# Channel mix after pooled attention: transposing the probabilities of tiles 6 to 35 as 32 by 32 blocks on VectorE, with on-chip transfers, instead of on TensorE

## The chip, the core and the metric

The kernel runs on one core of one Trainium2 chip. The metric is device time in microseconds (us). TensorE (PE in the profile, PEld for its weight loads) multiplies matrices, VectorE (DVE), ScalarE (ACT) and GpSimd (POOL) work on elements, and SyncE (SP) issues transfers. Each engine takes its own instructions strictly in order; an instruction that has to wait holds up all that stand behind it on its engine.

## The reference: what is computed

Eight batches of 576 tokens, 8 heads of width 64. Keys and values are averaged over groups of 8, so each head has 72 keys. Then attention, and a channel mix over the 512 attended features of each token and of the token before it:

```python
k_p = k.reshape(B, H, Sp, pool, D).mean(axis=3)
v_p = v.reshape(B, H, Sp, pool, D).mean(axis=3)
scores = scale * np.matmul(q, k_p.transpose(0, 1, 3, 2))
attn = softmax(scores)
x = np.matmul(attn, v_p)             # heads side by side: 8 x 576 x 512
xk = mu_k * x + (1.0 - mu_k) * x_prev
xr = mu_r * x + (1.0 - mu_r) * x_prev
k = np.maximum(xk @ w_k, 0.0)
v = k * k @ w_v
r = 1.0 / (1.0 + np.exp(-(xr @ w_r)))
out = r * v
```

## The kernel before

The 4608 tokens are cut into 12 chunks of 384 tokens, each of 3 tiles of 128 tokens: 36 tiles, numbered from 0. Line numbers here are those of the profile of the kernel before.

**Per tile.** `softmax` makes scores on TensorE (L592) into the one `sc` bank of PSUM, takes the maximum, subtracts, exponentiates on ScalarE (L628), sums and inverts on VectorE (L605 to L636), and multiplies by the inverse on GpSimd. It makes two tiles of this: `px` (L642), the last 8 keys of each head, and `pm` (L648), the first 64. The attention product needs the keys on the partitions. `transposed` does that for `pm` with four 128 by 128 TensorE transposes into a PSUM bank (L667), from which ScalarE copies a rounded high part `pth` (L678) and VectorE makes the low part `ptl` by subtraction (L680). `transposed_rest` spreads `px` on VectorE into three parts (L698, L700), transposes them with two TensorE instructions (L706), and ScalarE copies the result to `ptr` (L713).

**Per chunk.** `attended` (L749) multiplies values with `pth`, `ptl` and `ptr` into PSUM; `shifted` and `x_parts` make the mixed inputs `xkh`, `xkl`, `xrh`, `xrl` (L762 to L799). `hidden` (L825) multiplies with `w_k` in 8 groups, each into one of three `mm` banks that ScalarE (`rk`, `sh`) and VectorE (`rk`, `sl`) empty; `gate` (L874) multiplies with `w_r`, `mixed` (L906) with `w_v`, and each tile of outputs goes to memory from SyncE (L922). Except in chunk 0 each product is made of three matmuls, high with high, low with high, high with low. `pth`, `ptl` and `ptr` have one buffer each: a tile of chunk c may be written there only once chunk c-1 has been attended.

**What sets the order.** All steps are generators. `Order.run` plays them against a rough model of engine times and buffer slots, and records the instructions in the order in which this planner starts them; a step may begin when what it `need`s is `made` and the slot that it `take`s is free, and among the ready steps of an engine the one with the earliest due time wins. Attention steps on TensorE are held back by a `spare` of 3.0 us from chunk 2 on. `EARLIER` shifts single due times. The chip follows that order, whatever the times turn out to be. SyncE's one list holds all loads of queries, keys and values and the output stores.

Of the kernel before, what the change touches and what calls it, by code (L numbers as in the profile page):

```python
# [191 lines left out]
def attention_then_channel_mix(  # L192
# [60 lines left out]
    slots("xm", 3, [P, CH])  # L253
    slots("rk", 2, [P, CH])
    slots("e", 2, [P, 2, 4, KEYS])
    slots("pm", 2, [P, 2, 4, KM])
    slots("px", 2, [P, 2, 4, KR])
    slots("pr", 2, [P, 2, 3, 4, KR], F32R)
    slots("mx", 2, [P, 2, 4, 1])
    slots("sm", 2, [P, 2, 4, 1])  # L260
    slots("vq", 1, [REM, 2, D], F32R)
    slots("tmp", 2, [P, WP])
    slots("qs", 3, [P, NPAIR, P])
    slots("stage", 3, [P, 2 * POOL * KEYS])

# [63 lines left out]

    def warm():  # L330

        zeros = yield take("tmp")
        yield "dve", 0.5, False
        nc.vector.memset(zeros, 0.0)
        bank = yield take("bank")
        for _ in range(WARMING):
            yield "pe", 0.86, False
            nc.tensor.matmul(out=bank[:, :256], lhsT=zeros[:, :P], rhs=zeros[:, :256], start=True, stop=True)
        order.give("bank", bank)
        order.give("tmp", zeros)  # L340
# [74 lines left out]
    def convert(kind, i):  # L415

        yield need(("w" + kind, i))  # L420
        got = held.pop(("got", kind, i))
        w = got.rearrange("p (n two) -> p n two", two=2)
        low_word, top = w[:, :, 0], w[:, :, 1]
        ff = yield take("tmp")
        t = ff.bitcast(I32)
        yield act(WP)
        nc.scalar.activation(out=ff, in_=top.bitcast(F32), func=AF.Abs)
        yield "dve", 0.335, True
        nc.vector.tensor_scalar(out=ff, in0=ff, scalar1=TINY, scalar2=None, op0=ALU.max)  # L429
# [6 lines left out]
        nc.vector.scalar_tensor_tensor(  # L436
            out=t, in0=top, scalar=-0x40000000, in1=t, op0=ALU.bitwise_and, op1=ALU.bitwise_or
        )
        yield dve(WP)
        full[kind, i] = got[:, :WP].bitcast(F32)  # L440
        nc.vector.scalar_tensor_tensor(
            out=got[:, :WP], in0=low_word, scalar=29, in1=t,
            op0=ALU.logical_shift_right, op1=ALU.bitwise_or,
        )
        order.give("tmp", ff)
        order.make(("full", kind, i))

    order_of = [w[1:] for w in LOADS.split() if w[0] == "w"]
# [123 lines left out]
    def softmax(i):  # L572
# [61 lines left out]
            out=sm, in0=sm, scalar1=1e-9, scalar2=float(POOL), op0=ALU.add, op1=ALU.mult  # L634
        )
        nc.vector.reciprocal(out=sm, in_=sm)  # L636
# [5 lines left out]
        eng.tensor_tensor(  # L642
            out=px, in0=e[:, :, :, KM:], in1=sm.broadcast_to([P, 2, 4, KR]), op=ALU.mult
# [6 lines left out]
        )  # L650
        order.give("e", e)
        order.give("sm", sm)
        held["pm", i] = pm
        order.make(("pm", i))

    def transposed(i):
        c, off, _ = tiles[i]
        o = slice(off, off + P)
        yield need(("pm", i), *([("attended", c - 1)] if c else []))
        if c == 1:  # L660
            yield need(("early", "ptl", 0))
        pm = held.pop(("pm", i))
        bank = yield take("bank")
        tp = bank.rearrange("p (a b) -> p a b", b=P)
        yield "pe", 0.44, False
        for g in range(NPAIR):
            nc.tensor.transpose(  # L667
                out=tp[:, g, :],
                in_=pm[:, g // 2, (g % 2) * 2:(g % 2) * 2 + 2, :].rearrange("p h k -> p (h k)"),
                identity=ident,  # L670
            )
        order.give("pm", pm)
        yield act(NPAIR * P)
        if c in WHOLE:
            nc.scalar.copy(out=operand("pth", c)[:, :, o], in_=tp)
        else:
            pt_h, pt_l = operand("pth", c), operand("ptl", c)
            nc.scalar.copy(out=pt_h[:, :, o], in_=tp)  # L678
            yield dve(NPAIR * P, False)
            nc.vector.tensor_tensor(  # L680
                out=pt_l[:, :, o], in0=tp, in1=pt_h[:, :, o], op=ALU.subtract
            )
# [327 lines left out]
```

## Time and profile before

| | us |
|---|---|
| median of 3 runs (lowest, highest) | 635.99 (635.57, 636.23) |
| the profiled execution | 637.05 |
| its span, first to last instruction | 635.3 |
| TensorE busy | 621.9 |
| VectorE busy | 413.9 |
| ScalarE busy | 334.4 |
| GpSimd busy | 215.8 |

The 1.75 us between the span and the profiled execution lie around the program. Matmuls are pipelined, so the profile's time of one (277 ns for a transpose) is longer than what it adds to TensorE; what it adds is read from the starts of the instructions around it. "PE L667 x4" in a timeline is four instructions in a row of one line.

### The profile page before, as it was taken

The numbers are of one execution on the slowest core, as the hardware profiler recorded it, in microseconds if no ns is written. First come the engines' busy times: TensorE is split into PE (matmuls) and PEld (weight loads), VectorE is DVE, ScalarE is ACT, GpSimd is POOL, SyncE is SP. The second block draws the span as 40 slices with busy tenths as digits, with TensorE's granted clock in tenths as the row PEclk, the third lists the DMA queues.
The fourth block names the chain that finished last, engine by engine and source line by source line (L and its number), as shares of the span: only waits on it lengthen the run. The fifth ranks groups of instructions, "written<-read, shape, count | busy, mean of one in ns | idle before, by whom it ended". The sixth has DMA issues, their size and how long they took to land.

```text
span 635.3 us, 9068 instructions
## 1 busy us (share of the span) xinstructions
PE 621.9 (98%) x3256; PEld 538.6 (85%) x3256; DVE 413.9 (65%) x830; ACT 334.4 (53%) x688; POOL 215.8 (34%) x331
## 2 busy tenths in 40 slices
PE   7899999999999999999999999999999999999997
PEld 6754468889989989989988988988988988988986
DVE  5999998856979537647845665855854654653421
ACT  4667656855665644645454555546555455444420
POOL 1240348464435128028115018316405105203100
PEclk9999999999999999999999999999999999999999
DMA  9991130043314111033011061033110100000001
GB/s 293 364 390 62 33 125 35 15 126 142 91 51 172 61 35 51 0 142 108 17 35 51 0 202 49 16 109 125 33 34 34 35 17 34 18 0 35 18 0 50
DMA packets 35132, 50.91 MB, mean 80 GB/s; under 512 B 6544, under 2 KB 23184, under 8 KB 35088
## 3 DMA queue, kind: packets, MB, share of 16 engines
q1 hardware_dynamic: 34944, 50.22, 23.5%
q8 instruction: 25, 0.41, 0.3%
q14 instruction: 19, 0.16, 0.1%
q10 hardware_dynamic: 144, 0.13, 0.1%
HBM read 40.90 MB, written 9.44 MB: 79 GB/s over the span
## 4 chain that ended last, share of the span: by engine, by line
PE 84%; DMA 6%; DVE 5%; POOL 2%; SPq 1%; issue 1%; ACT 0%; DVEq 0%; POOLq 0%; ACTq 0%
PE mm L906 28%; PE mm L825 28%; PE mm L874 15%; PE bank L749 5%; PE sc L592 4%; DMA qs<-in_qT 4%; PE bank L667 2%; DMA got_wv<-in_w_v 1%; DMA got_wr<-in_w_r 1%; PE bank L706 1%; DVE tmp L436 1%; SPq L397 1%; POOL xkl L799 0%; DVE tmp L429 0%; POOL w_r L466 0%
## 5 line engine op out<-in xcount | busy, mean ns | idle before, releaser
L825 PE MATMUL mm<-xkh,w_k 128*128 128x384 f32 x704 | 182.2, 339 | 0.3 <-ACT xkh L797 0.3
L906 PE MATMUL mm<-w_v,sh 128*128 128x512 f32 x528 | 170.8, 392 | 0.0
L825 PEld LDWEIGHTS mm<-xkh,w_k 128*128 128x128 f32 x704 | 125.6, 188 | 1.5 <-issue 0.6
L825 PE MATMUL mm<-xkl,w_k 128*128 128x384 f32 x352 | 118.1, 336 | 0.7 <-POOL xkl L799 0.7
L906 PEld LDWEIGHTS mm<-w_v,sh 128*128 128x128 f32 x528 | 99.2, 188 | 19.8 <-issue 0.2
L906 PE MATMUL mm<-w_v,sl 128*128 128x512 f32 x264 | 103.0, 390 | 0.0
L642 POOL TENSOR_TENSOR px<-e,sm 128x64 f32<-128x64 f32 x32 | 11.4, 356 | 225.3 <-DVE sm L636 225.2
L874 PE MATMUL mm<-w_r,xrh 128*128 128x512 f32 x264 | 84.9, 394 | 0.0
L762 ACT ACTIVATE t<-bank,om_sb 128x384 f32<-128x384 f32 x96 | 48.8, 582 | 56.2 <-PE bank L749 56.1
L848 ACT CAST sh<-rk 128x384 fp32r<-128x384 f32 x88 | 45.2, 514 | 58.2 <-DVE rk L842 58.1
L781 DVE SCALAR_TENSOR_TENSOR xm<-bank,mu_sb,t 128x384 f32<-128x384 f32 x88 | 51.4, 612 | 35.2 <-POOL t L774 18.3
L850 DVE TENSOR_TENSOR sl<-rk,sh 128x384 fp32r<-128x384 f32 x88 | 53.5, 611 | 25.6 <-ACT sh L848 25.6
L825 PEld LDWEIGHTS mm<-xkl,w_k 128*128 128x128 f32 x352 | 66.1, 188 | 1.3 <-POOL xkl L799 1.3
L920 DVE TENSOR_TENSOR rs<-mm,rs 128x512 f32<-128x512 f32 (+1 forms) x37 | 24.8, 673 | 61.4 <-PE mm L906 61.4
L842 DVE SCALAR_TENSOR_TENSOR rk<-mm,rk 128x384 f32<-128x384 f32 x88 | 48.5, 553 | 16.4 <-ACT rk L835 15.8
L874 PEld LDWEIGHTS mm<-w_r,xrh 128*128 128x128 f32 x264 | 49.6, 188 | 10.0
L799 POOL TENSOR_TENSOR xkl<-xm,xkh 128x384 fp32r<-128x384 f32 x44 | 44.8, 1021 | 37.0 <-ACT xkh L797 36.6
L906 PEld LDWEIGHTS mm<-w_v,sl 128*128 128x128 f32 x264 | 49.7, 188 | 9.0
L473 POOL TENSOR_TENSOR stage<-stage 128x512 f32<-128x512 f32 (+5 forms) x60 | 51.0, 857 | 14.1 <-DMA stage<-in_vm 6.6
L835 ACT ACTIVATE rk<-mm 128x384 f32<-128x384 f32 x88 | 42.9, 488 | 23.3 <-PE mm L825 22.7
L874 PE MATMUL mm<-w_r,xrl 128*128 128x512 f32 x132 | 51.4, 389 | 0.0
L605 DVE TENSOR_REDUCE mx<-sc 128x8 f32<-128x576 f32 x35 | 26.3, 752 | 31.4 <-PE sc L592 31.4
(117 smaller groups left out, 979.2 us busy)
## 6 DMA issues: line engine op xcount, KB each, us to landing
out<-rs SPq DMA_DIRECT2D x35, 256.0 KB, 2.0
stage<-in_kT SPq DMA_DIRECT2D x15, 576.0 KB, 5.0
qs<-in_qT SPq DMA_DIRECT2D x32, 256.0 KB, 3.2
stage<-in_vm SPq DMA_DIRECT2D x14, 512.0 KB, 6.5
got_wk<-in_w_k SPq DMA_DIRECT2D x8, 512.0 KB, 9.2
got_wv<-in_w_v SPq DMA_DIRECT2D x8, 512.0 KB, 10.0
stage<-in_vr SPq DMA_DIRECT2D x7, 384.0 KB, 4.1
got_wr<-in_w_r SPq DMA_DIRECT2D x4, 512.0 KB, 8.3
```

The lines of the kernel that those rows point to most:

```text
L473: nc_eng.tensor_tensor(out=st[:, :, :w], in0=st[:, :, :w], in1=st[:, :, w:2 * w], op=ALU.add)
L749: nc.tensor.matmul(out=xp[:, o], lhsT=v, rhs=p, start=(q == 0), stop=(q == len(terms) - 1))
L762: nc.scalar.activation(out=t[:, m, 1:n + 1], in_=xp, func=AF.Copy, scale=om_sb[:, m, g:g + 1])
L781: nc.vector.scalar_tensor_tensor(out=xm[:, :n], in0=xp, scalar=mu_sb[:, m, g:g + 1], in1=t[:, m, :n], op0=ALU.mult, op1=ALU.add,)
L799: nc.gpsimd.tensor_tensor(out=lo, in0=xm[:, :n], in1=hi, op=ALU.subtract)
L825: nc.tensor.matmul(out=hp, lhsT=w[:, o], rhs=x[:, ct, :n], start=(ct == 0 and k == 0), stop=(ct == NCT - 1 and k == len(terms) - 1),)
L835: nc.scalar.activation(out=rk[:, :n], in_=hp, func=AF.Relu)
L842: nc.vector.scalar_tensor_tensor(out=rk[:, :n], in0=hp, scalar=0.0, in1=rk[:, :n], op0=ALU.max, op1=ALU.mult)
L848: nc.scalar.copy(out=sh[:, :n], in_=rk[:, :n])
L850: nc.vector.tensor_tensor(out=operand("sl", c)[:, jt, :n], in0=rk[:, :n], in1=sh[:, :n], op=ALU.subtract)
L874: nc.tensor.matmul(out=bank, lhsT=x[:, ct, o], rhs=w, start=(ct == 0 and k == 0), stop=(ct == NCT - 1 and k == len(terms) - 1),)
L906: nc.tensor.matmul(out=bank, lhsT=s[:, o], rhs=w, start=(jt == 0 and k == 0), stop=(jt == NJT - 1 and k == len(terms) - 1),)
```

## The change

For tiles 6 to 35, from the first tile of chunk 2 on, `transposed` and `transposed_rest` are not run. GpSimd multiplies all 72 keys of `e` in place in one instruction. A new step, `turned`, lets VectorE transpose 32 by 32 blocks in three instructions into `u` (in a slot of kind `pm`), and SyncE then issues 16 transfers from SBUF to SBUF, 4 for each quarter of the partitions, which put the blocks where a whole transpose would have put them, in `d` (a slot of kind `tmp`, of which there are two). Twelve of the transfers hold 32 rows of 512 bytes, four hold 32 rows of 768 bytes. A new step, `split_turned`, waits for the transfers and for chunk c-1 to be attended; ScalarE copies `pth` and twice a part of `ptr` out of `d`, VectorE subtracts for `ptl` and for the third part of `ptr`. Then `d` is free again. Only `warm` and `convert` are edited otherwise, for the new shape of `tmp`. The `EARLIER` entries for `transposed_rest 6` and `transposed_rest 8` have no step left to shift.

The core of the diff (renamings for the larger `pm` and `tmp` slots left out):

```diff
+TURNED = 6
+BLOCK = 32
...
-    slots("pm", 2, [P, 2, 4, KM])
+    slots("pm", 2, [P, 2 * 4 * KEYS])
...
-    slots("tmp", 2, [P, WP])
+    slots("tmp", 2, [P, P // BLOCK, 6 * BLOCK])
...
         eng = nc.vector if v else nc.gpsimd
+        if i >= TURNED:
+            yield dve(8 * KEYS) if v else pool(8 * KEYS)
+            eng.tensor_tensor(out=e, in0=e, in1=sm.broadcast_to([P, 2, 4, KEYS]), op=ALU.mult)
+            order.give("sm", sm)
+            yield from turned(i, e)
+            return
...
+    at_of = [0, 6 * BLOCK, 10 * BLOCK, 14 * BLOCK, 18 * BLOCK]
+
+    def turned(i, e):
+        u = yield take("pm")
+        yield "dve", 0.8, False
+        pairs = e.rearrange("p a (h two) k -> p (a h) two k", two=2)
+        for h2 in range(2):
+            lo, hi = at_of[2 * h2], at_of[2 * h2 + 2]
+            if h2 == 0:
+                hi = 2 * at_of[1]
+            nc.vector.transpose(
+                out=u[:, lo:hi].rearrange("p (f n) -> p f n", f=2)[:, :, :4 * BLOCK].rearrange(
+                    "p f (g j) -> p f g j", j=BLOCK
+                ),
+                in_=pairs[:, :, h2, :KM].rearrange("p g (f j) -> p f g j", j=BLOCK),
+            )
+        nc.vector.transpose(
+            out=u[:, 4 * BLOCK:6 * BLOCK].rearrange("p (r h k) -> p r h k", r=2, k=KR), in_=e[:, :, :, KM:]
+        )
+        order.give("e", e)
+        d = yield take("tmp")
+        for a in range(P // BLOCK):
+            yield "sp", 1.6, False
+            for c in range(4):
+                nc.sync.dma_start(
+                    out=d[c * BLOCK:(c + 1) * BLOCK, a, :at_of[c + 1] - at_of[c]],
+                    in_=u[a * BLOCK:(a + 1) * BLOCK, at_of[c]:at_of[c + 1]],
+                )
+        held["turned", i] = d
+        order.fetched(("turned", i), 400)
+        order.now += 3.0
+        order.give("pm", u)
...
+    def split_turned(i):
+        c, off, _ = tiles[i]
+        yield need(("turned", i), ("attended", c - 1))
+        d = held.pop(("turned", i))
...
+        yield act(NPAIR * P)
+        nc.scalar.copy(out=pt_h, in_=main)
+        yield act(2 * P)
+        nc.scalar.copy(out=ptr[:rows], in_=rest)
+        yield dve(NPAIR * P)
+        nc.vector.tensor_tensor(out=pt_l, in0=main, in1=pt_h, op=ALU.subtract)
+        order.make(("main", i))
+        yield dve(2 * P)
+        nc.vector.tensor_tensor(out=ptr[rows:2 * rows], in0=rest, in1=ptr[:rows], op=ALU.subtract)
+        yield act(2 * P)
+        nc.scalar.copy(out=ptr[2 * rows:], in_=rest)
+        order.give("tmp", d)
+        order.make(("side", i))
...
+        if i >= TURNED:
+            order.add(tile_due[i] + 0.1, split_turned(i), spare)
+            continue
         order.add(tile_due[i] + 0.1, transposed(i), spare)
         order.add(tile_due[i] + 0.1, transposed_rest(i), spare)
```

Line numbers of the changed kernel differ: L592 becomes L596, L825 L894, L874 L943, L906 L975, L835 and L848 (`rk` and `sh` on ScalarE) L904 and L917.

On TensorE, between the gates and the mixing of chunk 5, stood before: the end of the gates, the scores of tile 21, the two kinds of transposes of tile 20, the mixing.

```order
L874 MATMUL mm_116<-w_r_839,xrl_2426 128x512
L874 MATMUL mm_116<-w_r_839,xrh_2425 128x512
L592 MATMUL sc_112<-kbd_69,qs_103 128x144 x4
L667 MATMUL bank_113<-ident,pm_90 128x128 x4
L706 MATMUL bank_115<-ident,pr_94 96x128 x2
L906 MATMUL mm_118<-w_v_939,sh_2551 128x512
L906 MATMUL mm_118<-w_v_939,sl_2582 128x512
```

The same place now:

```order
L943 MATMUL mm_116<-w_r_846,xrl_2631 128x512
L943 MATMUL mm_116<-w_r_846,xrh_2630 128x512
L596 MATMUL sc_112<-kbd_70,qs_105 128x144 x4
L975 MATMUL mm_118<-w_v_867,sh_2742 128x512
L975 MATMUL mm_118<-w_v_867,sl_2784 128x512
```

The transposes are gone, and the scores are those of tile 23: from here to the end of the scores each tile is scored two tiles earlier against the chunks than before, so that chunk 6 is attended (after 24 matmuls of the mixing that begins here) when its last tile, 20, was scored a whole chunk ago. At the start the other thing has moved: chunk 2 is attended after 36 matmuls of the mixing of chunk 1, where it was 24 before.

On ScalarE, in the hidden products of chunk 5, stood before, at the fifth to the eighth group (`pth`, `ptr` here from a PSUM bank):

```order
L678 CAST pth_2525<-bank_114 128x4x128
L713 CAST ptr_2608<-bank_115 96x2x128
L848 CAST sh_2551<-rk_86 128x384
L835 ACTIVATE rk_87<-mm_118 128x384
L848 CAST sh_2551<-rk_87 128x384
L835 ACTIVATE rk_86<-mm_117 128x384
```

The same place now (L742, L744 and L751 are the copies out of the transferred blocks):

```order
L904 ACTIVATE rk_86<-mm_116 128x384
L917 CAST sh_2742<-rk_86 128x384
L742 CAST pth_2671<-tmp_102 128x4x128
L904 ACTIVATE rk_87<-mm_118 128x384
L744 CAST ptr_2673<-tmp_102 32x2x128
L917 CAST sh_2742<-rk_87 128x384
L904 ACTIVATE rk_86<-mm_117 128x384
L751 CAST ptr_2673<-tmp_102 32x2x128
```

The three copies of one tile now stand between the fifth and the seventh emptying of an `mm` bank, and the first of them waits for transfers.

On SyncE, past the middle of the program, the transfers of a tile stand in one list with the loads and stores; each of them also waits for the transfer eight places ahead of it. With the semaphores that each waits for (`DMAHW0` to `DMAHW7` are the transfers' own):

```order
L692 DMA tmp1_102<-pm0_90 32x192 [waits DMAHW7_49,DVE_49,Activation_49]
L692 DMA tmp1_102<-pm0_90 32x128 [waits DMAHW0_49]
L692 DMA tmp1_102<-pm0_90 32x128 [waits DMAHW1_49]
L692 DMA tmp1_102<-pm0_90 32x128 [waits DMAHW2_49]
L692 DMA tmp1_102<-pm0_90 32x192 [waits DMAHW3_49]
L692 DMA tmp1_102<-pm0_90 32x128 [waits DMAHW4_49]
L692 DMA tmp1_102<-pm0_90 32x128 [waits DMAHW5_49]
L692 DMA tmp1_102<-pm0_90 32x128 [waits DMAHW6_49]
L692 DMA tmp1_102<-pm0_90 32x192 [waits DMAHW7_49]
```

Before, nothing but loads and stores stood there. Of the third tile of one chunk the last eight transfers stand behind a load of queries, two of keys and one of values:

```order
L692 DMA tmp_102<-pm_90 32x128 x3
L392 DMA qs_105<-in_qT 128x4x128
L414 DMA stage_107<-in_kT 128x1152
L414 DMA stage_106<-in_kT 128x1152
L414 DMA stage_108<-in_vm 128x1024
L692 DMA tmp_102<-pm_90 32x192
```

The loads have moved between the two halves of a tile's transfers.

More of the change, by code (lines that the diff above doesn't have):

```diff
@@ L330, in warm @@
     def warm():
-        zeros = yield take("tmp")
+        got = yield take("tmp")
+        zeros = got.rearrange("p a n -> p (a n)")
         yield "dve", 0.5, False
-        nc.vector.memset(zeros, 0.0)
+        nc.vector.memset(zeros[:, :WP], 0.0)
         bank = yield take("bank")
@@ L339, in warm @@
         order.give("bank", bank)
-        order.give("tmp", zeros)
+        order.give("tmp", got)
     def fill(after, times):
@@ L423, in convert @@
         low_word, top = w[:, :, 0], w[:, :, 1]
-        ff = yield take("tmp")
+        spare = yield take("tmp")
+        ff = spare.rearrange("p a n -> p (a n)")[:, :WP]
         t = ff.bitcast(I32)
@@ L444, in convert @@
         )
-        order.give("tmp", ff)
+        order.give("tmp", spare)
         order.make(("full", kind, i))
@@ L636, in softmax @@
         nc.vector.reciprocal(out=sm, in_=sm)
-        px = yield take("px")
-        pm = yield take("pm")
         v = NORM_BY.get(i, "g") == "v"
         eng = nc.vector if v else nc.gpsimd
+        if i >= TURNED:
[4 more added lines that the diff above has]
+            return
+        px = yield take("px")
+        got = yield take("pm")
+        pm = got[:, :8 * KM].rearrange("p (a h k) -> p a h k", a=2, h=4)
         yield dve(8 * KR) if v else ("pool", 0.24, True)
@@ L652, in softmax @@
         order.give("sm", sm)
-        held["pm", i] = pm
+        held["pm", i] = got, pm
         order.make(("pm", i))
+    at_of = [0, 6 * BLOCK, 10 * BLOCK, 14 * BLOCK, 18 * BLOCK]
[29 more added lines that the diff above has]
+        order.give("pm", u)
     def transposed(i):
@@ L661, in transposed @@
             yield need(("early", "ptl", 0))
-        pm = held.pop(("pm", i))
+        got, pm = held.pop(("pm", i))
         bank = yield take("bank")
@@ L671, in transposed @@
             )
-        order.give("pm", pm)
+        order.give("pm", got)
         yield act(NPAIR * P)
@@ L684, in transposed @@
         order.make(("main", i))
+    def split_turned(i):
+        c, off, _ = tiles[i]
+        yield need(("turned", i), ("attended", c - 1))
+        d = held.pop(("turned", i))
+        split_by = lambda t: t.rearrange("p g (a j) -> p g a j", j=BLOCK)
+        o = slice(off, off + P)
+        main = d[:, :, :4 * BLOCK].rearrange("p a (g j) -> p g a j", j=BLOCK)
+        rest = d[:4 * KR, :, 4 * BLOCK:].rearrange("p a (r j) -> p r a j", j=BLOCK)
+        pt_h, pt_l = split_by(operand("pth", c)[:, :, o]), split_by(operand("ptl", c)[:, :, o])
+        ptr, rows = split_by(operand("ptr", c)[:, :, o]), 4 * KR
+        yield act(NPAIR * P)
[11 more added lines that the diff above has]
+        order.make(("side", i))
     def transposed_rest(i):
```

## The prediction

> **What bounds the kernel now.** I read the page's busy times and chain first, then the stretches, then TensorE's own timeline.
>
> ```profile
> PE 621.9 (98%) x3256; PEld 538.6 (85%) x3256; DVE 413.9 (65%) x830; ACT 334.4 (53%) x688; POOL 215.8 (34%) x331
> ...
> PE 84%; DMA 6%; DVE 5%; POOL 2%; SPq 1%; issue 1%; ACT 0%; DVEq 0%; POOLq 0%; ACTq 0%
> PE mm L906 28%; PE mm L825 28%; PE mm L874 15%; PE bank L749 5%; PE sc L592 4%; DMA qs<-in_qT 4%; PE bank L667 2%; DMA got_wv<-in_w_v 1%; DMA got_wr<-in_w_r 1%; PE bank L706 1%; DVE tmp L436 1%; SPq L397 1%; POOL xkl L799 0%; DVE tmp L429 0%; POOL w_r L466 0%
> ```
>
> The chain that ends last is TensorE for 84%; the transposes (L667, L706) are on it with 2% and 1%. The stretches tell where: the first row is the time in which chunk 1 begins, the second the sum of ten stretches of 50 us from 130 to 630 us.
>
> ```profile
> 103.00:131.00 28.00, 27.71 (x150) 25.22 (x151) 21.60 (x44) 20.35 (x43) 14.49 (x15) 1.00 0.18 44
> ...
> sum 500.00, PE 500.00 PEld 452.27 DVE 299.18 ACT 252.22 POOL 168.35; mean PE 50.00 PEld 45.23 DVE 29.92 ACT 25.22 POOL 16.84
> ```
>
> From 103 us to the end TensorE has no idle time, at the full clock (1.00). Whatever leaves TensorE's list there shortens the run, if nothing else comes late. VectorE has 40% of that time free, ScalarE half.
>
> **What is removed from TensorE.** Its timeline at one tile's transposes:
>
> ```profile
> 216.83 0.60 PE L667 MATMUL bank<-ident,pm 128*128 128x128 f32 x4
> 217.26 0.38 PE L706 MATMUL bank<-ident,pr 128*96 128x128 f32 x2
> 217.40 0.48 PE L874 MATMUL mm<-w_r,xrh 128*128 128x512 f32 x1
> 217.72 0.39 PE L874 MATMUL mm<-w_r,xrl 128*128 128x512 f32 x1
> 217.95 0.63 PE L874 MATMUL mm<-w_r,xrh 128*128 128x512 f32 x2
> 218.41 0.39 PE L874 MATMUL mm<-w_r,xrl 128*128 128x512 f32 x1
> 218.64 0.62 PE L874 MATMUL mm<-w_r,xrh 128*128 128x512 f32 x2
> ```
>
> I count starts, since ends are modelled. Three matmuls of the gate take 218.64 - 217.95 = 0.69, 0.23 each. From 216.83 to 217.95 are 1.12: two such matmuls (0.46) and six transposes, so 0.66 a tile. The first of the thirty tiles stands here, past 103 us:
>
> ```profile
> 104.63 0.60 PE L667 MATMUL bank<-ident,pm 128*128 128x128 f32 x4
> ```
>
> So all thirty count: 19.8 us.
>
> **What VectorE, ScalarE and GpSimd lose and gain**, per tile, first the removed groups, then the nearest rows for what comes:
>
> ```profile
> L698 DVE CAST pr<-px 128x64 fp32r<-128x64 f32 x72 | 28.1, 433 | 5.8 <-POOL px L642 5.8
> L700 DVE TENSOR_TENSOR pr<-px,pr 128x64 fp32r<-128x64 f32 x36 | 9.2, 260 | 0.0
> L680 DVE TENSOR_TENSOR ptl<-bank,pth 128x512 fp32r<-128x512 f32 x33 | 22.5, 686 | 7.3 <-ACT pth L678 7.2
> L678 ACT CAST pth<-bank 128x512 fp32r<-128x512 f32 x33 | 19.1, 583 | 16.9 <-PE bank L667 16.8
> L713 ACT CAST ptr<-bank 96x256 fp32r<-96x256 f32 x36 | 13.3, 370 | 0.2 <-PE bank L706 0.2
> L642 POOL TENSOR_TENSOR px<-e,sm 128x64 f32<-128x64 f32 x32 | 11.4, 356 | 225.3 <-DVE sm L636 225.2
> L648 POOL TENSOR_TENSOR pm<-e,sm 128x512 f32<-128x512 f32 x32 | 34.1, 1065 | 0.0
> ...
> L559 DVE TENSOR_TENSOR vbd_r<-vq,mask_sb 96x256 fp32r<-96x256 f32 x16 | 6.0, 417 | 0.2
> L466 DVE TENSOR_TENSOR w_k<-got_wk,w_k 128x512 fp32r<-128x512 f32 x4 | 2.8, 688 | 0.0
> L463 ACT CAST w_k<-got_wk 128x512 fp32r<-128x512 f32 x8 | 4.9, 615 | 3.0 <-POOL w_k L466 2.8 <-DVE w_k L466 0.2
> L537 ACT CAST vbd_h<-vbd_w 128x256 fp32r<-128x256 f32 x2 | 0.7, 408 | 0.0
> ```
>
> VectorE loses 2 x 0.433 + 0.260 + 0.686 = 1.81. It gets the subtraction out of SBUF (0.69 as L466), the one of 256 elements (0.42 as L559), and three block transposes that no trace shows: by element count two like L559 and one like L700, 0.42 + 0.42 + 0.26 = 1.10. Together 2.21, 0.4 more a tile, 12 us in all, in an idle share of 200 of 500 us. If a block transpose costs four times that, 3.3 more a tile, 99 us, it still fits; if it costs nothing, VectorE gains 0.7 a tile, which shortens nothing. ScalarE loses 0.95 and gets 0.62 + 2 x 0.41 = 1.43: 14 us more, into half free time. GpSimd loses 1.42 for one instruction between 1.07 and 1.42: no cost. None of these touches the sum; they count where an engine waits in order.
>
> **The transfers on SyncE.** How long an issue keeps SyncE, how long a transfer takes to land, what SyncE waits for now:
>
> ```profile
> 191.12 0.35 SPq L922 DMA_DIRECT2D out<-rs  x1
> 191.57 0.54 SPq L389 DMA_DIRECT2D qs<-in_qT  x1
> 192.17 1.12 SPq L411 DMA_DIRECT2D stage<-in_kT  x2
> ...
> out<-rs SPq DMA_DIRECT2D x35, 256.0 KB, 2.0
> stage<-in_kT SPq DMA_DIRECT2D x15, 576.0 KB, 5.0
> early_xrl<-in_vm SPq DMA_DIRECT2D x1, 512.0 KB, 10.4
> ...
> SPq L922 <- DVE rs L920: 252.0, 32, 33.9
> ```
>
> An issue costs 0.35 to 0.56. The new ones have plain rows of 512 or 768 bytes, nearest to the stores: 0.35. Sixteen: 5.6 us, up to 9.0. Landing: 2.0 as the stores, to 5.0 behind loads of keys, and 10.4 in the crowd at the start. So a tile's blocks are there 7.6 us after VectorE is done, 14 behind loads. SyncE now mostly waits (252 us for outputs alone).
>
> Is that hidden? A chunk's period on TensorE, from scores to the next chunk's scores at the same place:
>
> ```profile
> 313.80 0.98 PE sc L592 x8
> ...
> 363.14 0.98 PE sc L592 x8
> ```
>
> 49.3 us before, 47.3 after. SyncE needs 48 x 0.35 = 17 us of that, and some 4 for loads and stores. And by the new order a chunk's last tile is scored a whole chunk before it is attended, so 14 us of latency are covered from chunk 4 on. If that cover went, TensorE would stand up to 14 us a chunk.
>
> Chunk 2 has no such lead; its last tile is the first place to look:
>
> ```profile
> 115.01 1.04 POOL L648 TENSOR_TENSOR pm<-e,sm 128x512 f32<-128x512 f32 x1
> ...
> 126.43 5.50 PE mm L906 x24
> ```
>
> Tile 8 is ready on GpSimd at 116.1; transposed 117.2; issued 122.8 to 126.2; landed 124.8 to 131.2; copied and subtracted (0.62 + 0.41 + 0.42, and handing over, 1.6) 126.4 to 132.8. TensorE starts mixing at 126.4, less three tiles' transposes (2.0) 124.4, and attends after 36 matmuls of 0.23, at 132.7. Slack 6.3 to -0.1: nothing lost, taking the stores' price.
>
> **What may be lost in order.** ScalarE's first copy of a tile waits for the transfers with the emptying of an `mm` bank (L835) queued behind it, and TensorE waits for that bank; VectorE's subtraction queues in the same way. What an emptying and the way to the next chunk's products cost:
>
> ```profile
> L762 ACT ACTIVATE t<-bank,om_sb 128x384 f32<-128x384 f32 x96 | 48.8, 582 | 56.2 <-PE bank L749 56.1
> ...
> L781 DVE SCALAR_TENSOR_TENSOR xm<-bank,mu_sb,t 128x384 f32<-128x384 f32 x88 | 51.4, 612 | 35.2 <-POOL t L774 18.3 <-POOL xkl L799 6.9 <-POOL t L770 6.1
> ...
> L799 POOL TENSOR_TENSOR xkl<-xm,xkh 128x384 fp32r<-128x384 f32 x44 | 44.8, 1021 | 37.0 <-ACT xkh L797 36.6
> ...
> L835 ACT ACTIVATE rk<-mm 128x384 f32<-128x384 f32 x88 | 42.9, 488 | 23.3 <-PE mm L825 22.7 <-DVE sl L850 0.2
> ```
>
> Where the last eight transfers follow three loads they may come 3 us late. TensorE has two further banks, two groups of 12 matmuls of 384 columns (0.23 x 3/4 = 0.17 each, 4.2 us together), less 1.1 for the emptying on ScalarE (0.49) and VectorE (about 0.61 as L781): it loses what exceeds 3.1 us. At the stores' landing that is nothing, behind loads about nothing. At a chunk's end two such copies (2 x 1.03) also stand among ScalarE's casts for the next chunk's first products, where the cover is 21 mixing matmuls and a score, 5.8 us, against a path of 2 x 0.58 (L762) + 0.61 + 0.5 (a cast, as L835) + 1.02 = 3.3, with the copies 5.4, and some hand-overs: up to 0.3 a chunk. I allow 1.0 us in all, between 0 and 2.7.
>
> **The sum.** 637.05 (profiled execution) - 19.8 + 1.0 = 618.2. The median is 1.06 below the profiled execution: 617.2.
>
> **The rivals.**
>
> *ScalarE's wait empties the banks* (ends slower). Transfers that land as late as the row of 10.4, not 2.0, in every chunk: the third tile's copy is 8.4 late, TensorE loses 8.4 - 3.1 = 5.3 a chunk, over ten chunks 53: 617 + 53 = 670. It decides from 2.0 us beyond the slack of 3.1: 19.8 over ten chunks. For it: 480 transfers share their queue with all loads. Against: between 103 and 131 us the transfer engines are 18% busy (the 0.18 in the row of that stretch). 5%. A mild form, 4.1 late, costs 1.0 a chunk: 627. 8%.
>
> *The transfers do not overlap* (slower). If each had to land before the next is issued, a tile would take 16 x 2.0 = 32 us, a chunk 96 and 4 for the rest against 47.3: ten chunks 527 longer, 1144 us. SyncE decides the time from (47.3 - 4) / 48 = 0.90 us a transfer. Against: the second load of keys at 192.17 is issued 0.56 after the first, which lands after 5.0; the order waits only for the transfer eight places ahead, and eight issues (2.8) outlast a landing of 2.0. 3%. The Trainium skill's page "DMA: Bandwidth & Descriptors", section "Rules for kernel authors", speaks against this change: many small transfers should be made one large one, since under 64 KB one pays mostly overhead. These have 16 or 24 KB. By that rule the 2.0 us would be overhead paid 16 times, if it could not overlap; the trace agrees that 2.0 is paid for landing, but shows landings side by side.
>
> *The start slips.* Tile 8's blocks land at 10.4: 5.7 us late at the first attention of chunk 2, once, and perhaps in part at chunk 3: 620 to 623. 14%.
>
> *No change.* Stalls of 0.66 a tile would just eat the gain: 636. 2%. That the transposes stay is excluded: the order has none for these tiles.
>
> **How the numbers follow.** The forecast (616 to 620) has 68%, the late start 14%, the mild wait 8%, no change 2%, the two slow cases 8%. About 0.2% is what a measurement can tell here. The range: below, the full 19.8 and 0.7 for spread, 615.5; above, 624, past the late start; left out are the mild wait beyond it, no change and the slow cases, 18%. Faster 90%, same 2%, slower 8%.
>
> **What would show it.** Right: no L667 or L706 after tile 5, TensorE without idle time from 103 us, its period 47.3, SyncE's issues at 0.35, the transfers' landing near 2. Wrong: TensorE waiting for `rk` on ScalarE, with ScalarE's `pth` copy waiting for DMA (the mild or the heavy wait), a long wait of TensorE at chunk 2 alone (the start), or SyncE issuing without a break (transfers as the bound).

## The result: 0.9% slower

The changed kernel takes 641.73 us (median of four runs, 640.62 to 642.95), the kernel before 636.06 in the same comparison: ratio 1.0091, 95% interval 1.0072 to 1.011. The forecast was 617.2, between 615.5 and 624.0. The profiled execution takes 641.90 us, 4.85 more than that of before.

### The profile page after: what moved, and what is told of

Read it like the earlier page. It is cut to its first block, busy times and chain, and to the rows that moved or that the text cites. A ratio compares the mean times of both kernels' runs of the same rounds, so it can differ in the third digit from the quotient of the medians.

```text
span 640.1 us, 9422 instructions
## 1 busy us (share of the span) xinstructions
PE 611.4 (96%) x3076; PEld 522.6 (82%) x3076; DVE 425.0 (66%) x860; ACT 344.7 (54%) x718; POOL 216.1 (34%) x301
## 4 chain that ended last, share of the span: by engine, by line
PE 49%; DMA 17%; DVE 15%; SPq 9%; ACT 3%; issue 3%; POOL 2%; DVEq 0%; ACTq 0%; POOLq 0%
PE mm L975 19%; PE mm L894 15%; PE mm L943 11%; SPq L692 8%; DMA qs<-in_qT 7%; DMA tmp<-pm 4%; PE bank L818 3%; DMA stage<-in_vm 3%; PE sc L596 2%; DVE ptl L746 2%; DVE sl L919 2%; DVE rk L911 2%; DMA got_wv<-in_w_v 2%; DMA out<-rs 1%; DMA got_wr<-in_w_r 1%
## 5 line engine op out<-in xcount | busy, mean ns | idle before, releaser
L894 PE MATMUL mm<-xkh,w_k 128*128 128x384 f32 x704 | 185.5, 345 | 11.7 <-DVE rk L911 10.1
L975 PE MATMUL mm<-w_v,sh 128*128 128x512 f32 x528 | 171.3, 393 | 3.3 <-ACT rs L950 3.1
L894 PEld LDWEIGHTS mm<-xkh,w_k 128*128 128x128 f32 x704 | 128.5, 192 | 16.8 <-DVE rk L911 13.8
L894 PE MATMUL mm<-xkl,w_k 128*128 128x384 f32 x352 | 120.3, 342 | 1.4 <-POOL xkl L868 1.3
L975 PEld LDWEIGHTS mm<-w_v,sh 128*128 128x128 f32 x528 | 99.2, 188 | 24.4 <-ACT rs L950 3.7
L645 POOL TENSOR_TENSOR e<-e,sm 128x576 f32<-128x576 f32 x30 | 35.8, 1195 | 210.9 <-DVE sm L640 194.5
L975 PE MATMUL mm<-w_v,sl 128*128 128x512 f32 x264 | 103.1, 390 | 0.0
L943 PE MATMUL mm<-w_r,xrh 128*128 128x512 f32 x264 | 84.2, 394 | 0.0
L917 ACT CAST sh<-rk 128x384 fp32r<-128x384 f32 x88 | 45.0, 512 | 63.5 <-DVE rk L911 63.5
L919 DVE TENSOR_TENSOR sl<-rk,sh 128x384 fp32r<-128x384 f32 x88 | 54.9, 626 | 28.4 <-ACT sh L917 28.0
L894 PEld LDWEIGHTS mm<-xkl,w_k 128*128 128x128 f32 x352 | 67.5, 192 | 3.4 <-POOL xkl L868 3.4
L477 POOL TENSOR_TENSOR stage<-stage 128x512 f32<-128x512 f32 (+5 forms) x60 | 55.6, 932 | 12.7 <-DMA tmp<-pm 7.0
L943 PEld LDWEIGHTS mm<-w_r,xrh 128*128 128x128 f32 x264 | 49.6, 188 | 10.7 <-issue 0.4
L975 PEld LDWEIGHTS mm<-w_v,sl 128*128 128x128 f32 x264 | 49.7, 188 | 9.0
L943 PE MATMUL mm<-w_r,xrl 128*128 128x512 f32 x132 | 51.4, 390 | 0.0
L904 ACT ACTIVATE rk<-mm 128x384 f32<-128x384 f32 x88 | 42.5, 486 | 13.8 <-PE mm L894 13.0
L868 POOL TENSOR_TENSOR xrl<-xm,xrh 128x384 fp32r<-128x384 f32 x44 | 45.2, 1030 | 0.9 <-ACT xrh L866 0.7
```

The lines of the kernel that those rows point to most:

```text
L477: nc_eng.tensor_tensor(out=st[:, :, :w], in0=st[:, :, :w], in1=st[:, :, w:2 * w], op=ALU.add)
L868: nc.gpsimd.tensor_tensor(out=lo, in0=xm[:, :n], in1=hi, op=ALU.subtract)
L894: nc.tensor.matmul(out=hp, lhsT=w[:, o], rhs=x[:, ct, :n], start=(ct == 0 and k == 0), stop=(ct == NCT - 1 and k == len(terms) - 1),)
L904: nc.scalar.activation(out=rk[:, :n], in_=hp, func=AF.Relu)
L917: nc.scalar.copy(out=sh[:, :n], in_=rk[:, :n])
L919: nc.vector.tensor_tensor(out=operand("sl", c)[:, jt, :n], in0=rk[:, :n], in1=sh[:, :n], op=ALU.subtract)
```

## The profile after

Busy times and the chain that ended last, from the page of the changed kernel:

```profile
PE 611.4 (96%) x3076; PEld 522.6 (82%) x3076; DVE 425.0 (66%) x860; ACT 344.7 (54%) x718; POOL 216.1 (34%) x301
...
PE 49%; DMA 17%; DVE 15%; SPq 9%; ACT 3%; issue 3%; POOL 2%; DVEq 0%; ACTq 0%; POOLq 0%
PE mm L975 19%; PE mm L894 15%; PE mm L943 11%; SPq L692 8%; DMA qs<-in_qT 7%; DMA tmp<-pm 4%; PE bank L818 3%; DMA stage<-in_vm 3%; PE sc L596 2%; DVE ptl L746 2%; DVE sl L919 2%; DVE rk L911 2%; DMA got_wv<-in_w_v 2%; DMA out<-rs 1%; DMA got_wr<-in_w_r 1%
```

TensorE has 180 instructions fewer (30 tiles x 6), but the chain runs over it for 49% where it was 84%; 26% of it are now SyncE's issues and what they move, loads included. The stretches that were shown of before, and one more (columns as there; the last three are the granted clock, the share of the transfer engines and GB/s):

```profile
103.00:131.00 28.00, 24.31 (x119) 21.98 (x118) 21.09 (x43) 18.35 (x39) 11.27 (x10) 0.94 0.11 29
180.00:230.00 50.00, 43.85 (x220) 38.75 (x219) 33.53 (x72) 23.59 (x47) 13.43 (x20) 0.93 0.28 88
...
sum 500.00, PE 488.16 PEld 435.73 DVE 310.14 ACT 264.16 POOL 170.11; mean PE 48.82 PEld 43.57 DVE 31.01 ACT 26.42 POOL 17.01
```

TensorE stands idle for 11.8 of the 500 us past 130, where it was never idle before, and in two places its clock is below 1.00. Added up between the starts of its matmuls past 100 us, gaps of over 0.3 us are 19.5 us, against 1.1 before; three stretches of 3.4 us at half clock cost up to another 5.1 (two of them begin while TensorE still idles). The change was to take 19.8 off 637.05; up to 18.4 + 5.1 = 23.5 of the 24.65 that are missing lie in these two sums. Most of it falls in two places: from hidden products to hidden products chunk 1 takes 56.4 us where it took 51.2, and chunk 3, in which tiles 12 to 14 are copied, 57.2 where it took 48.4.

One such gap, in the hidden products of a chunk, from the timeline of the changed kernel (start, length, engine, line; in brackets the idle time before the instruction and what ended it):

```profile
204.38 0.60 SPq L392 DMA_DIRECT2D qs<-in_qT  x1
205.03 1.09 SPq L414 DMA_DIRECT2D stage<-in_kT  x2
206.22 0.38 SPq L414 DMA_DIRECT2D stage<-in_vm  x1
206.69 0.48 SPq L991 DMA_DIRECT2D out<-rs  x1
207.22 10.71 SPq L692 DMA_DIRECT2D tmp<-pm  x12
...
219.13 0.62 ACT L742 CAST pth<-tmp 128x512 fp32r<-128x512 f32 x1 [6.24 <-DMA tmp<-pm]
219.78 0.69 DVE L746 TENSOR_TENSOR ptl<-tmp,pth 128x512 fp32r<-128x512 f32 x1 [5.85 <-ACT pth L742]
220.91 0.49 ACT L904 ACTIVATE rk<-mm 128x384 f32<-128x384 f32 x1
221.44 0.56 DVE L911 SCALAR_TENSOR_TENSOR rk<-mm,rk 128x384 f32<-128x384 f32 x1 [0.38 <-ACT rk L904]
222.05 1.01 PE L894 MATMUL mm<-xkh,w_k 128*128 128x384 f32 x2 [3.43 <-DVE rk L911]
```

Read upwards it is the first rival's chain: TensorE waits for a bank, the bank for `rk`, `rk` for ScalarE, which stood 6.24 us at the `pth` copy of tile 13, and that for transfers that SyncE was issuing until 217.9. Tile 13 is the second tile of its chunk, not the third, of which the prediction speaks. Two things add up here. The sixteen issues themselves take some 11.0 us with the pauses between them. Four loads and a store between them take 2.45, and SyncE stands another 2.6 until loads of keys and values have landed, because each transfer waits for the one eight places ahead; the first transfer behind the loads landed 7.8 us after its issue. Without those 5 us, an estimate, the copy would have stood some 1.2 us, too little to reach TensorE. But with half the issues (e3 below) the same loads and store stand among tile 13's transfers, and its copy does not wait; and other gaps have no loads in them: for the one at 109.8, tile 6's sixteen issues stand in a row from 98.8 to 109.2. Over the run, from the table of waits (in total, times, longest):

```profile
ACT pth L742 <- DMA tmp<-pm: 42.9, 18, 6.2
DVE ptl L746 <- ACT pth L742: 15.0, 7, 5.8
PE mm L894 <- DVE rk L911: 10.1, 7, 3.4
```

The new instructions themselves, first SyncE's issues (shortest, median, longest in ns), then how long from issue to landing (the median of those of 16 KB; then shortest, median and longest of all), then groups of instructions:

```profile
L692 SPq DMA_DIRECT2D tmp<-pm x480: 507/588/1840, 98.8 to 561.6; - x160
```

```profile
tmp<-pm SPq DMA_DIRECT2D x360, 16.0 KB, 1.8
```

```profile
DMA to landing us min/median/max: 1.7/1.8/7.8
```

```profile
L678 DVE STREAM_TRANSPOSE pm<-e 128x256 f32<-128x256 f32 x60 | 22.9, 420 | 12.5 <-POOL e L645 12.5
L742 ACT CAST pth<-tmp 128x512 fp32r<-128x512 f32 x30 | 18.5, 622 | 42.9 <-DMA tmp<-pm 42.9
L684 DVE STREAM_TRANSPOSE pm<-e 128x64 f32<-128x64 f32 x30 | 6.0, 201 | 0.0
```

Block transposes, copies and the median landing are about what the forecast took (0.42, 0.26, 0.62, 2.0). The issue is not: 0.59 where it took 0.35. From a tile's first issue to the end of its sixteenth are 10.0 to 16.1 us, over 30 tiles, not 5.6; the six over 12 us have three or more loads or stores in between.

## The experiments

**Theory 1**: an issue takes 0.63 us with its pause, the planner counts 0.40, so ScalarE's copy stands in the order ahead of the landing, and TensorE pays. **Rivals**: the transfers' traffic slows others (2); the work added on VectorE and ScalarE delays operands (3); issuing engines pay (4); any new order of the instructions costs (5); the tile with which the change begins makes the difference (6).

### e1: SyncE's price in the plan

```
-            yield "sp", 1.6, False
+            yield "sp", 2.6, False
```

> The changed kernel, with the planner told 2.6 us for four transfers on SyncE instead of 1.6; nothing else differs, so only the recorded order changes. Theory 1 (issues take 0.63 us each instead of the 0.40 that the planner counts, so the blocks come 3 us or more after ScalarE's place for copying them, and ScalarE stands there with the emptying of TensorE's banks queued behind it): the copies move to later places, TensorE's waits for rk shrink from 24 us to under 8, and the time falls from 641.7 to 618-627. Rival 2 (the transfers' traffic slows the other engines): no change, 640-643. Rival 3 (the extra work on VectorE and ScalarE delays the products' operands): 638-643.

641.42 us (639.92 to 642.04), ratio 1.0081 (1.0062 to 1.01): nothing gained. Its waits:

```profile
DVE pm L678 <- DMA tmp<-pm: 8.8, 9, 1.9
...
ACT pth L742 <- DMA tmp<-pm: 6.4, 5, 4.7
```

ScalarE's wait fell from 42.9 to 6.4 us, TensorE's waits for `rk` (with those of its weight loads) from 23.9 to 17.9 where under 8 was expected, its idle time only from 19.5 to 18.6. Theory 1 in this simple form falls: a part of the waits moved to VectorE, whose block transposes now stand for a buffer from which earlier transfers still read.

### e2: the same order without transfers

```
-        u = yield take("pm")
+        slot = yield take("pm")
+        d = yield take("tmp")
+        u = d.rearrange("p a n -> p (a n)")
...
-                nc.sync.dma_start(
-                    out=d[c * BLOCK:(c + 1) * BLOCK, a, :at_of[c + 1] - at_of[c]],
-                    in_=u[a * BLOCK:(a + 1) * BLOCK, at_of[c]:at_of[c + 1]],
-                )
```

> The changed kernel without the 480 transfers: VectorE writes its blocks straight into the tile that ScalarE and VectorE then copy and subtract, so the probabilities stay in the wrong places. TensorE, ScalarE and GpSimd have the same instructions in the same order; some of VectorE's block transposes stand a few places later. Theory 1: the waits go with the transfers, 616-620. Rival 2 (traffic): the same number, 616-620. Rival 3 (extra work on VectorE and ScalarE, or the new order itself): the time stays above 630.

629.83 us (626.71 to 631.3), ratio 0.9896 (0.9863 to 0.9928), between what the theories said: idle time past 100 us 9.3. About half of the loss goes with the transfers. Some block transposes had to move and now wait for the one pair of buffers left, so the rest is not all the extra work's.

### e3: half the issues, the same bytes

```
-            for c in range(4):
+            for c in range(a % 2, 4, 2):
...
-                    out=d[c * BLOCK:(c + 1) * BLOCK, a, :at_of[c + 1] - at_of[c]],
+                    out=d[c * BLOCK:(c + 1) * BLOCK, a0:a0 + 2, :n],
```

> The changed kernel with 8 transfers a tile instead of 16, each twice as large: one block row is sent to two places, so the same bytes land, but half of the probabilities are replaced by copies of others. Order unchanged. Theory 1 (the number of issues counts): issues of about 0.6 us, blocks some 5 us earlier, ScalarE's wait for transfers falls from 43 us to under 12, 618-625. Rival 2 (the traffic counts): 640-643. A third reading of the issue's price, that it goes by the pieces in a transfer and not by the transfer: issues of 1.0 to 1.2 us, 640-643.

625.29 us (624.99 to 625.64), ratio 0.9831 (0.9816 to 0.9846). The issues:

```profile
L693 SPq DMA_DIRECT2D tmp<-pm x240: 585/594/1861, 98.3 to 540.2; - x120
```

This is 0.3 us above theory 1's range and far from that of rival 2. ScalarE never waits for a transfer now. With the same instructions in the same order on the four other engines, half the issues are worth 641.7 - 625.3 = 16.4 us: the number of transfers to issue counts, not the bytes. An issue with twice the pieces costs the same 0.59. TensorE still idles 7.6 us, 6.3 of them between 100 and 165.

### e4: idle transfers in the kernel before

```
         held["pm", i] = pm
+        if i >= 6:
+            idle()
```

> The kernel before, with 16 idle transfers for each tile from the seventh on, put on SyncE where GpSimd has normalized the tile; they have the shapes of the changed kernel's, move constants from one tile to another, and nobody waits for them. Theory 1 (only the wait in ScalarE's order costs): 635.5-637.5. Rival 2 (traffic on the ports and queues slows the others): above 645, spread over all chunks. Rival 3 says nothing of it (636). The price of an issue by itself: 0.51 for one after a rest and 0.59 in a row, as in the changed kernel.

654.78 us (654.31 to 655.06), ratio 1.0294 (1.0278 to 1.0309): a miss for both, since theory 1 expected 636 and rival 2 a loss spread over all chunks. It is one gap of 15 us. SyncE and VectorE there:

```profile
200.95 11.20 SPq L666 DMA_DIRECT2D idle_to<-idle_from  x16
212.25 0.60 SPq L390 DMA_DIRECT2D qs<-in_qT  x1
212.95 1.04 SPq L412 DMA_DIRECT2D stage<-in_kT  x2
```

```profile
216.92 0.76 DVE L474 TENSOR_TENSOR stage<-stage 128x576 f32<-128x576 f32 x1 [17.11 <-DMA stage<-in_kT]
```

The loads of keys, issued at 192.17 before, stood behind idle transfers until 212.95; VectorE stood 17.1 us for them. The clock adds to it (stretches of this kernel):

```profile
205.00:220.00 15.00, 1.48 (x10) 1.18 (x8) 3.08 (x6) 0.00 (x0) 0.00 (x0) 0.67 0.48 159
220.00:230.00 10.00, 8.69 (x35) 8.64 (x36) 8.67 (x20) 5.94 (x15) 1.65 (x2) 0.64 0.31 89
```

(1 - 0.67) x 15 + (1 - 0.64) x 10 = 8.6 us of full clock are missing, half of 17.1 at half clock. But these 17.1 us begin at 210.1, and TensorE stood idle until 221.3; only the 5.9 us left then slow it, by 2.9. 15 + 2.9 is 17.9 of the 18.7 us lost. So what stands behind transfers on SyncE pays, and traffic does not. The theory gets this second part.

### e5: from tile 15 on

```
-TURNED = 6
+TURNED = 15
```

> The changed kernel, turning only from tile 15 on (the chunk after the one in which the second batch's keys are loaded), so 21 tiles. Theory 1, now narrower (SyncE's list is full in the first chunks: each tile's transfers take it 10 us, and what stands behind them, further blocks and the loads of keys, comes late; in the first chunks VectorE has no time to spare either): the loss of chunks 1 and 3 goes, the gain of 21 x 0.66 = 13.9 us stays less some 0.7 us a chunk, 622-628. Rival 2 (each tile's transfers cost the other engines something wherever they stand): 21/30 of the loss of 5.6 is left, 638-642.

646.74 us (646.23 to 647.31), ratio 1.0172 (1.0157 to 1.0187): slower than with all tiles, a plain miss. A wait and a stretch of it:

```profile
ACT pth L742 <- DMA tmp<-pm: 61.3, 14, 7.0
```

```profile
295.00:310.00 15.00, 11.75 (x62) 11.43 (x61) 9.49 (x17) 5.99 (x15) 9.45 (x11) 0.89 0.21 65
```

At 301.1 ScalarE's copy has stood 6.44 us, and TensorE 3.25; up to 1.7 more go with the clock (0.11 x 15). The tile is 19, again the second of its chunk; its sixteen issues stand in a plain row of 10.0 us, with no load between them, and the last lands 1.2 after that. From chunk 5 to chunk 9 a chunk takes 51.7 to 52.5 us from hidden products to hidden products, where before it took 49.1 to 50.0. SyncE began each tile's transfers at once or, behind those of the tile before, within 7 us, so its list kept up: the copy simply stands too early. That spoke for the plan's prices, and against the start as the cause.

### e6 and e8: every second group of four issued elsewhere

```
-                nc.sync.dma_start(
+                (nc.gpsimd if a % 2 else nc.sync).dma_start(
```

e8 has `nc.scalar` in that place.

> The changed kernel with every second group of four transfers issued by GpSimd instead of SyncE; all transfers are made, in the same recorded order. Theory 1 (SyncE's list): a tile's issues take 5 us on SyncE beside 5 on GpSimd, as with half the issues, 624-631. Rival 2 (bytes, or the landing): 639-643. Rival 4 (GpSimd, held up by issuing, delays its subtractions xkl and the normalizing): its own work comes late and the time is above 632.

> The changed kernel with every second group of four transfers issued by ScalarE instead of SyncE, in the same recorded order. ScalarE gets 8 issues of 0.5 to 0.6 us a tile, 4.4 us, 13 a chunk, in order ahead of its copies and emptyings. Theory 1 (SyncE's list): SyncE is relieved as with GpSimd, but ScalarE, 80% busy in chunk 1, pays: 628-638. Rival 2 (bytes or landing): 640 or more.

e6: 639.75 us (639.2 to 640.18), ratio 1.0061 (1.0046 to 1.0076). e8: 678.37 (677.36 to 679.69), ratio 1.067 (1.0653 to 1.0688). Both are above theory 1's range. By the number alone rivals 2 and 4 both fit, each time; the traces decide for rival 4. A place in e6:

```profile
205.44 1.98 POOL L692 DMA_DIRECT2D tmp<-pm  x4
207.44 1.16 POOL L645 TENSOR_TENSOR e<-e,sm 128x576 f32<-128x576 f32 x1
```

```profile
208.63 0.45 DVE L678 STREAM_TRANSPOSE pm<-e 128x256 f32<-128x256 f32 x1 [1.95 <-POOL e L645]
```

GpSimd issues (0.50 each) ahead of the next tile's normalizing, VectorE's transposes wait for that, and TensorE, through `xm` and the `xkh` made of it, idles 2.6 us from 208.4 on. ScalarE's wait for transfers is gone (0.6 us), so it is not late landings that cost here. In e8 ScalarE issues ahead of its emptyings, and TensorE idles 51 us.

The Trainium skill, page "DMA: Bandwidth & Descriptors", section "Issuing engines are not separate DMA queues", says that issuing on several engines only saves the time to initiate, usually small relative to the DMA itself. Here one issue takes 0.59 us of the 1.8 from issue to landing, and since landings overlap and issues do not, sixteen take 10.0, so the "usually small" does not hold in these runs; but where it goes, another engine's list pays.

### e7: idle transfers from tile 15 on, in three shapes

```
-        if i >= 6:
-            idle()
+        if i >= 15:
+            idle(i)
```

> The kernel before with idle transfers again, but only from tile 15 on, 336 of them, in three shapes: for seven tiles 32 rows to other partitions as in the change, for seven 32 rows to the same partitions, for seven 128 rows to the same partitions (four times the bytes). Theory 1 (only loads that stand behind them on SyncE cost): no load of keys that is needed soon stands behind them, 635.5-638. Rival 2 (traffic): a loss in proportion to their number, 645 or more. The price of an issue: 0.51 to 0.59 us for the first shape; if the shift of partitions makes it dear, 0.33 to 0.4 for the second; if the few rows do, 0.33 to 0.4 for the third alone.

680.73 us (678.49 to 681.2), ratio 1.0695 (1.0673 to 1.0717), the largest miss, by a fault of the experiment: the third shape's transfers write the same place, four in a row, so most waited for the one before to land (84 waits of SyncE, 124 us in all). SyncE issued 32 of them in 51.68 us, outputs stood behind, and TensorE idled 33 us from 570 on and 7 from 649 on. The first two shapes, 224 transfers from 204 us on, answer the question; of seven stretches of 50 us the first and the last, by which the third shape has begun:

```profile
205.00:255.00 50.00, 50.00 (x278) 45.49 (x277) 27.90 (x58) 25.69 (x53) 21.14 (x35) 1.00 0.23 64
...
505.00:555.00 50.00, 50.00 (x279) 45.30 (x278) 27.50 (x55) 24.40 (x47) 13.15 (x26) 1.00 0.22 66
```

TensorE is busy 50.00 of 50 at the full clock, in all seven: the traffic of such transfers costs it nothing, rival 2 is out. With or without a shift of partitions an issue is 0.51 after a pause and 0.59 in a row; with 128 rows and 64 KB it is 0.46 and 0.60.

### e9: less work on VectorE in the first chunks

```
-        for h2 in range(2):
+        for h2 in range(2 if i >= 12 else 0):
```

(on e3, with two small memsets at the start)

> The kernel with half the issues (e3) in which VectorE also leaves out the two larger block transposes of tiles 6 to 11, 0.84 us a tile, 5.0 in all; what the transfers move is then old. Everything else stands in the same order. It asks what the 7.6 us are that TensorE still idled there. Theory 1, its second part (VectorE, 80 to 90% busy between 93 and 165 us, has no room for 0.4 us a tile and delays the operands): the idle time falls to under 4 us and the time from 625.3 to 620-623. Rival 5 (the new order of the instructions, not their length): 624.5-626.

624.58 us (623.22 to 625.12), ratio 0.9807 (0.9788 to 0.9825). Idle time between 100 and 165 fell from 6.3 to 4.1 us; the time fell by less than the intervals tell apart. Theory 1 missed both its figures, narrowly for the idle time, and the time lies in rival 5's range. VectorE's load seems to have a part in the last 8 us; how large a part, and whether the order has the rest, stays open.

### e10 to e12: versions that do the whole work, with measured prices

The planner is told 2.6 for four issues, and in `turned` and `split_turned`:

```
-        yield "dve", 0.8, False
+        yield "dve", 1.0, False
...
-        yield act(NPAIR * P)
+        yield "act", 0.6, False
...
-        yield act(2 * P)
+        yield "act", 0.4, False
...
-        yield dve(NPAIR * P)
+        yield "dve", 0.65, True
...
-        yield dve(2 * P)
+        yield "dve", 0.42, True
```

The tiles are `i >= 6 and i % 3 != 2` in e10, `i >= 12` in e11, `i >= 6 and i % 3 == 1` in e12.

> A kernel that does the whole work: of each chunk's three tiles, from the seventh tile on, the first two go by blocks and transfers and the third by TensorE, and the planner is told the measured prices (2.6 us for four issues, 1.0 for the block transposes, 0.6, 0.4 and 0.4 for ScalarE's copies, 0.65 and 0.42 for the subtractions). Theory 1 (SyncE's list and the two buffers on either side of the transfers are too short for three tiles a chunk): 20 tiles x 0.66 = 13.2 us gained, 6 to 8 lost at the start, a little later: 628-632. Rival 5 (any new order costs more than the gain): 638 or more.

> The changed kernel, turning all tiles from the thirteenth on (24 tiles) with the planner told the measured prices as in e10. Gain 24 x 0.66 = 15.8. Theory 1: VectorE's loss in the first chunks is gone, SyncE still has three tiles a chunk: a stall of 1 to 3 us in some chunks where VectorE or ScalarE stands for a transfer, 624-634, and below 640 in any case. Rival 2 (a cost for each transfer wherever it stands, as in the run from tile 15 on): 643 or more.

> As e10, but only the second of each chunk's three tiles goes by blocks and transfers, ten tiles: 6.6 us less on TensorE, 160 transfers. Theory 1: hardly a wait for transfers, 629.5-633. Rival 5 (the new order): 637 or more.

e10: 630.4 us, ratio 0.9896 (0.9878 to 0.9915); e11: 625.49, 0.9817 (0.9798 to 0.9837); e12: 633.09, 0.9951 (0.9934 to 0.9968). e10 and e11 are in theory 1's ranges, e12 is 0.1 us above its own. Rival 5 falls: three new orders, and each gains.

### e13 to e16: prices against the start

e13 is e5 with e11's prices; e14 is e11 with the old prices; e15 is the change as made (`i >= 6`) with e11's prices; e16 is e14 with 2.6 for four issues alone.

> Turning from tile 15 on, as in e5, but with the planner told the measured prices. Theory 1 (with a wrong price the planner puts ScalarE's copy ahead of the landing of the third tile in each chunk): ScalarE's wait for transfers falls from 61 us to under 15, the gaps of 3 us and the half clock behind them go, and the time falls from 646.7 to 623-629. Rival 6 (the starting tile makes the difference between e5 and e11): 640 or more.

> Turning from tile 12 on, as in e11, but with the planner's old prices. Theory 1: ScalarE stands 3 us for the third tile's transfers in most chunks, 636-648. Rival 6 (the starting tile): 624-628, as e11.

> The change as made, from tile 6 on, with the planner told all measured prices (e1 had only that of SyncE). Theory 1, with its part on the first chunks (there VectorE and SyncE's list are full, so that the right price moves the loss instead of removing it): 632-641. If wrong prices are all there is: 620-627.

> As e11, from tile 12 on, but only SyncE's price is changed (2.6 us for four issues), the prices of the copies and transposes are the old ones. Theory 1 says that SyncE's price is the one that matters: 623-628. If the prices on ScalarE and VectorE matter as much: 632 or more.

| begins with | old prices | SyncE's price | all prices |
|---|---|---|---|
| tile 6 | 641.73, 1.0091 (1.0072 to 1.011) | e1: 641.42, 1.0081 (1.0062 to 1.01) | e15: 635.82, 0.9985 (0.9971 to 0.9999) |
| tile 12 | e14: 634.31, 0.997 (0.9957 to 0.9984) | e16: 627.7, 0.9856 (0.9836 to 0.9876) | e11: 625.49, 0.9817 (0.9798 to 0.9837) |
| tile 15 | e5: 646.74, 1.0172 (1.0157 to 1.0187) | | e13: 624.16, 0.9796 (0.978 to 0.9813) |

The same edit is 1.7% slower or 2.0% faster from tile 15 on, by the prices alone. The wait and the stretch of e5, in e13:

```profile
ACT pth L742 <- DMA tmp<-pm: 5.7, 2, 3.0
```

```profile
295.00:310.00 15.00, 14.90 (x87) 14.59 (x86) 14.57 (x26) 8.79 (x21) 8.88 (x10) 1.00 0.17 50
```

TensorE idles 1.7 us in all past 100 us, and 12.3 of the 21 x 0.66 = 13.9 arrive. From tile 12 on SyncE's price alone brings 6.6 of the 8.8 us between e14 and e11. e14 missed both ranges, theory 1's (636 to 648) by a little: its order has one gap of 5.7 us and few others, so what a wrong price costs depends on where it lets the copies fall, and with the old prices the starting tile makes a difference too. From tile 6 on the right prices help only from 641.7 to 635.8, and 10.3 of the 14.7 us of e15's idle time lie between 100 and 170:

```profile
131.00:165.00 34.00, 28.69 (x143) 24.97 (x142) 26.76 (x50) 18.43 (x40) 21.20 (x26) 0.95 0.43 135
```

and the same stretch of the kernel before:

```profile
131.00:165.00 34.00, 34.00 (x188) 31.84 (x187) 24.79 (x47) 19.11 (x41) 16.34 (x23) 1.00 0.34 113
```

There VectorE is busy for 26.8 of 34 us (24.8 before) and a tile's transposes wait for buffers and for GpSimd: at the start the loss moves, it does not go. About half of e1's idle time (9 of 18.6 us) lies between 100 and 170 too; the other half lies in smaller gaps behind it.

## Why the prediction was wrong, point by point

- **The bound and the gain**: right. TensorE was the bound, and 0.66 us a tile is there to be had; e13 gets 0.59 a tile.
- **The price of an issue**: this step failed, and with it the direction of the change. "The new ones have plain rows of 512 or 768 bytes, nearest to the stores: 0.35. Sixteen: 5.6 us, up to 9.0." The rows in the profile were stores that SyncE issues after a pause of 1 to 34 us; a transfer costs 0.51 after a pause, 0.59 in a row and 0.63 with the pause between two, so sixteen take 10.0, outside both bounds. Even stores, in the changed kernel, take 0.37 to 0.56 directly behind another issue (15 of them) against a median of 0.34 after a pause (21). Where nothing stands between, the blocks are there 11.3 us after VectorE (10.0, and 1.2 from the end of the last issue to its landing), not 7.6, nor the 9.4 for which the order was made (four groups of 1.6, and 3.0).
- **"Slack 6.3 to -0.1: nothing lost, taking the stores' price"**: nothing was lost at that place, though not for the reason given. Tile 8's transfers, behind those of tile 7, are issued from 120.7 to 130.7; its last part is ready at 135.1, and chunk 2 is attended at 137.8, later than the 132.7 of the forecast, without idle time before it. The loss came earlier, at tile 6's copy among the emptyings of chunk 1 (the gap at 109.8).
- **"TensorE ... loses what exceeds 3.1 us"**: the rule was right. 6.24 of waiting gave 3.43 of idle time, 6.44 in e5 gave 3.25. What was wrong was what went into it: "at the stores' landing that is nothing". The first rival had the right chain; its cause, landings as late as 10.4 in every chunk, is not what happened (median 1.8, longest 7.8 us): the issues in a row are, in places with loads between them. It was given 5% and, mild, 8%.
- **Three loads ahead of a tile's last transfers**: "they may come 3 us late", "behind loads about nothing". The lateness was of that order (5 us in the gap shown, for four loads and a store); on top of issues that had used up the cover it was no longer nothing.
- **What no step had**: an idle time of TensorE may be followed by 3.4 us at half clock, up to 1.7 more; up to 5.1 in all.
- **VectorE, "in an idle share of 200 of 500 us"**: an average. The row of the first chunks (21.60 of 28 us busy before) was in the profile. With half the issues (e3) TensorE still lost 6.3 us there; e9 puts some of that on VectorE.
- **"If each had to land before the next is issued"**: they overlap, as forecast. The rule of the Trainium skill, page "DMA: Bandwidth & Descriptors", section "Rules for kernel authors" (make many small transfers one large one), points the right way all the same: e3 moves the same bytes with half the transfers and is 16.4 us faster, though what is saved is SyncE's issuing, not the landing.
- **Start, or no change**: the late start was real (chunk 1 takes 5.2 us longer), as one part of the loss; chunk 3, with 8.8, is the larger.

Open: the last 8 us of e3 are only partly explained, and why the old prices hurt from tile 15 more than from tile 12 was not traced beyond where the waits fall.

## What to carry to other kernels

Price an issue from a row of issues, not from one that follows a rest, and multiply it by their number before asking whether the landing is hidden. When a step moves to another queue in a planned order, give the plan the measured price first: an engine that works in order and stands a few microseconds too early for a buffer can cost more than the step that was saved. An average idle share says nothing of the stage in which the new work falls.

## What the runs showed of the hardware

- An issue on SyncE from one on-chip tile to another costs 0.59 to 0.60 us in a row, whether it moves 16, 32 or 64 KB in 32 or 128 rows (the changed kernel, e3, e7); after a pause it is 0.51 for 16 KB, 0.59 for 32 KB in two pieces, 0.46 for 64 KB. GpSimd takes 0.50 (e6).
- The traffic of such transfers costs TensorE nothing (e7: more than 224 of them in 350 us without a gap); what stands behind them in the same list is late (e4).
- TensorE's clock is halved for 3.4 us or a multiple of it (6.8 in e14, 10.2 in e8, 17.1 in e4), at moments that lie whole multiples of 3.41 us apart within a run. What decides, in these runs, is how long TensorE stood idle between two such moments (gaps of over 0.3 us added up): from 100 us on, over all 18 kernels, each of the 19 halvings follows 3.41 us with 2.0 us or more of idle time, and none follows 3.41 us with 1.9 or less. So a gap of 1.5 us with smaller ones beside it (2.1 in all, at 205 to 208 in the changed kernel) was enough, and in e5 a gap of 2.99 was not, because it fell into two such stretches with 1.4 and 1.6. The Trainium skill's page "TensorE: Matmul & The Clock Gate", section "What's actually happening", tells of a free-running window of 3413 ns and of half rate after an idle one. The length and the fixed beat agree (3.4, 6.8, 10.2 and 17.1), but here a window that was idle for 60% sufficed.
